# Pooled attention and two gated layers on one core: the first pair's stack is built in place, and three groups of transfers and conversions change their places

## The chip, the cores and the metric

One core of a Trainium2 chip runs the whole program in one launch. The metric is the device time of one execution in microseconds (us); lower is better. The kernel before was timed in three runs, and a fourth execution was taken by the hardware profiler.

## What is computed

Inputs are q, k, v of shape (4, 8, 1152, 64) and two pairs of weight matrices. The reference, cut to what matters:

```python
q_pool = q.reshape(B, H, S // 2, 2, D).mean(axis=3)          # 576 pooled queries per head
scores = scale * matmul(q_pool, k^T)                          # 576 x 1152 per head
scores = scores - max(scores, axis=-1)
attn = exp(scores); attn = attn / (sum(attn) + 1e-09)
x = matmul(attn, v), laid out as 2304 tokens x 512
h = x @ w1_in;  x = (h - tanh(h)) @ w1_out                    # 512 -> 2048 -> 512
h = x @ w2_in;  y = (h * sigmoid(1.702 * h)) @ w2_out         # the same shape
```

## The kernel before, in words

**Attention.** The 32 heads are taken as 16 pairs (`NPAIR`), two heads (s = 0 and 1) to a pair. Of each operand a rounded high part and the rest, the low part, are kept, so that a product is made of three matmuls. Each head has a *stack*, one of three buffers `stacks[h % 3]` = (a1, a2, q2, q3): a1 holds the high part of k on partitions 0 to 63 and the low part on 64 to 127, a2 the high part of k with a row of ones, q2 the high part of the pooled q twice, q3 its low part and, as its 65th row, the negated row of maxima. `stack(p, s)` (L308) fills the four with six transfers on SP's queue, 1296 KB in all, out of the pair's tiles kh, kl, qh, ql.

A pair is 18 steps (`NS`), a head 9 of them, one for each 128 keys. Step g issues `scores(g)` (four matmuls, L392 and L393; the last kind reads a2 and q3 and with it the row of maxima), two exponentials on ACT (L398 and L408; only the first in every third step, which is called whole), the subtraction of the high from the full probabilities on DVE or POOL (`rest`, L416), and `pv(g - 3)` (L428, L438). Beside these run the maxima of the next pair (`max_tile`, L324 on PE and L328 on DVE), which `max_rows(p, s)` (L345) transposes on DVE into `tt` and writes with four small transfers into q3. `prep_*`, `load_*`, `sums`, `merge`, `spread` and `normalise` are hung on steps by the tables `plan` and, for pair 0, `opening`. An entry (o, i): job means: at step i of a pair, do it for the pair o further on. All engines and queues run in the order in which the program issues. SP takes its transfers in that order, and one that waits holds those behind it.

**The opening.** Pair 0 has nobody ahead of it. Its q and k come in halves of 64 partitions. `first_max` (L331) makes the maxima of head 0 in five tiles ahead of step 0 (three matmuls of 384 columns and one reduction of 1152 each), then one whole tile of head 1. The other four tiles of head 1 are cut into halves of 576, eight in all, at steps 0 to 2. `keep_warm` (L566) puts matmuls between whose result nobody reads. `sum_q(1)` (L279), which needs the load of pair 1's q, stands at step 0 on DVE, and `prep_qs(2)`, which needs that of pair 2's, at step 5.

**The two layers** are 80 steps of 24 + 24 matmuls (L691 and L786): 2 layers x 4 quarters of the weights x 5 blocks of tokens (384, 512, 512, 512, 384) x 2. `gate` (L715) makes the activation on ACT and DVE, and `split_g(n)` (L697) splits it into a high part on ACT and a low part, on POOL in layer 0 and on DVE in layer 1. The weights come as 64-bit numbers: each of the 8 pieces of a quarter is converted by four DVE instructions (L137, L143, L150, L157) and one split. The table `turn`, or `usual`, names the step in which a piece is converted (`cv`) and split (`sp`); its load is issued two steps earlier. `split_x` (L112) splits the input blocks of a layer.

Of the kernel before, what the change touches and what calls it, by code (L numbers as in the profile page):

```python
# [28 lines left out]
def tile_pooled_attention_two_moe(  # L29
# [14 lines left out]
    D = 64  # L44
# [166 lines left out]
    def attention(ctx: ExitStack):  # L211
# [119 lines left out]
        def first_max(s, j, x, pool, parts, n):  # L331
            d = pairs[0]
            r = slice(64 * s, 64 * s + 64)
            m = min(128, SP - 128 * j)
            mx = pool.tile([128, parts, 512], F32, tag="mx", name="mx")
            for a in range(parts):
                k0 = (x * parts + a) * n
                nc.tensor.matmul(
                    mx[0:m, a, 0:n], d["qh"][r, 128 * j:128 * j + m], d["kh"][r, k0:k0 + n],
# [5 lines left out]
        def max_rows(p, s, queues=(nc.sync,) * 4):  # L345
# [7 lines left out]
            elif s == 1:  # L353
                nc.vector.tensor_tensor(
                    mt[:, 6:10], f32(mt[:, 6:10]), f32(mt[:, 22:26]), op=ALU.min)
# [13 lines left out]

        def prep_v(p, s):  # L370
            vr = vraw.pop((p, s))
            vr = vr.rearrange("p (m r) d -> p m r d", r=2)
            vh, vl = (outer(x) for x in vt[(2 * p + s) % 3])
            nc.sync.dma_start(
                out=vfs[(2 * p + s) % 3][:, :, 0:D],
                in_=v[p // NPB, p % NPB][:, s, 2 * KG:KT])
# [142 lines left out]
        load_q(0, [low])  # L519
        load_k(0, [low])  # L520
        load_q(0, [high])
        load_k(0, [high])
        load_k(1)
        fill(0)
        new_pair(0)
        d0 = pairs[0]

        def q_sum(eng, out, r):
            eng.tensor_add(d0[out][r], qraw[0][r, 0], qraw[0][r, 1])

        def k_high(eng, r, x):
            c = slice(x * SP, (x + 1) * SP)
            if eng is nc.scalar:
                eng.activation(d0["kh"][r, c], kraw[0][r, c], AF.Copy)
            else:
                eng.tensor_scalar(
                    out=d0["kh"][r, c], in0=kraw[0][r, c],
                    scalar1=1.0, scalar2=1.0, op0=ALU.mult, op1=ALU.mult)

        def k_low(r, x):  # L540
            c = slice(x * SP, (x + 1) * SP)
            nc.gpsimd.tensor_tensor(
                d0["kl"][r, c], kraw[0][r, c], f32(d0["kh"][r, c]), op=ALU.subtract)

        q_sum(nc.vector, "qh", low)
        k_high(nc.scalar, low, 0)
        k_high(nc.gpsimd, low, 1)
        q_sum(nc.vector, "qs", low)
        nc.vector.tensor_sub(d0["ql"][low], d0["qs"][low], f32(d0["qh"][low]))
        k_low(low, 0)  # L550
        k_low(low, 1)
        stack(0, 0)
        k_high(nc.scalar, high, 0)
        k_high(nc.scalar, high, 1)
        q_sum(nc.gpsimd, "qs", high)
        refill(1)
        nc.scalar.activation(d0["qh"][high], d0["qs"][high], AF.Copy)
        k_low(high, 0)
        k_low(high, 1)
        nc.gpsimd.tensor_tensor(  # L560
            d0["ql"][high], d0["qs"][high], f32(d0["qh"][high]), op=ALU.subtract)
        with (tc.tile_pool(name="ps_first", bufs=2, space=PSUM) as ps_first,
              tc.tile_pool(name="ps_warm", bufs=1, space=PSUM) as ps_warm):
            warm = ps_warm.tile([128, 512], F32, name="warm")

            def keep_warm(n):  # L566
                for _ in range(n):
                    nc.tensor.matmul(
                        warm, bdqs[1][:, 0:128], bdqs[1][:, 0:512], start=True, stop=True)
# [16 lines left out]
        prep_v(0, 1)  # L586
        prep_kl(1, 0)
        prep_kl(1, 1)
        load_v(1, 0)
        load_v(1, 1)  # L590
        load_k(2)
        nc.gpsimd.memset(f32(bdqs[0][:]), 0.0)
# [304 lines left out]
```

## Time and profile before

| | |
|---|---|
| three timed runs | 1322.97, 1324.94 (median), 1329.85 us |
| the profiled execution | 1328.51 us, of it 1326.7 us between first and last instruction |
| PE busy | 1297.1 us, 98% of the span |
| DVE, ACT, POOL busy | 988.9, 750.6 and 360.5 us |
| mean granted TensorE clock | 0.992 |
| DMA | 117.57 MB moved |

The span falls into an opening (to about 17 us no scores are made), the attention (to about 522 us) and the two layers (to the end). PE is TensorE's matmuls, PEld its weight loads, DVE VectorE, ACT ScalarE, POOL GpSimd, SP SyncE, which issues most transfers. A `q` behind an engine's name is its sequencer. In a timeline row stand the start, the duration, engine, line, operation, and in brackets how long the engine stood idle before it and for whom.

### The profile page before, as it was taken

What the parts mean: (1) busy time and instruction counts of PE and PEld (TensorE: products, weight loads), DVE (VectorE), ACT (ScalarE), POOL (GpSimd) and SP (SyncE); (2) the same over time, 40 slices, a digit from 0 to 9 for tenths busy, and PEclk for the clock granted to TensorE, in tenths of its full rate; (3) what the DMA queues carried; (4) which work ended last, traced back from release to release, by engine and by line L of the source; (5) the groups of instructions that cost most, each with busy time, mean ns of one, the idle gap of its engine ahead of it and who ended that gap; (6) DMA issues with size and microseconds to landing.
All of it is one profiled execution on the core that took longest, in us unless ns stands there. A gap on an engine that the chain in (4) does not pass through costs nothing.

```text
span 1326.7 us, 18918 instructions
## 1 busy us (share of the span) xinstructions
PE 1297.1 (98%) x7036; PEld 1156.0 (87%) x7036; DVE 988.9 (75%) x1279; ACT 750.6 (57%) x1151; POOL 360.5 (27%) x273
## 2 busy tenths in 40 slices
PE   7899999999999999999999999999999999999998
PEld 5799999999999998888879879889888888889887
DVE  6577877788888878998999999999844546545433
ACT  4567777777677767866666566665544322322211
POOL 4633333224344414223333332323210110110000
PEclk8899999999999999999999999999999999999999
DMA  8777666777877641111111110111211111211012
GB/s 175 182 165 165 149 148 154 173 184 160 186 168 169 160 116 35 42 48 48 48 48 33 48 48 32 49 31 41 72 33 32 53 43 34 62 33 32 24 40 80
DMA packets 59162, 117.57 MB, mean 89 GB/s; under 512 B 25024, under 2 KB 29120, under 8 KB 59072
## 3 DMA queue, kind: packets, MB, share of 16 engines
q1 hardware_dynamic: 59044, 116.38, 35.1%
q8 instruction: 55, 0.90, 0.3%
q14 instruction: 35, 0.29, 0.1%
q10 hardware_dynamic: 28, 0.00, 0.0%
HBM read 66.58 MB, written 4.79 MB: 54 GB/s over the span
## 4 chain that ended last, share of the span: by engine, by line
PE 65%; DVE 16%; DMA 9%; ACT 6%; issue 3%; POOL 1%; SPq 1%; DVEq 0%; POOLq 0%; ACTq 0%
PE y L786 20%; PE h L691 19%; PE pv L438 8%; PE pv L428 5%; PE sc L393 4%; PE sc L392 4%; PE mx L324 4%; DMA kr<-in_k_dram 2%; DVE gg L749 2%; DMA q<-ql 2%; DMA a<-kh 2%; DVE wt L143 2%; DVE wt L137 2%; DVE xb L799 2%; ACT u L730 2%
## 5 line engine op out<-in xcount | busy, mean ns | idle before, releaser
L328 DVE TENSOR_REDUCE mt<-mx 128x1 fp32r<-128x576 f32 x270 | 203.7, 755 | 92.5 <-PE mx L324 88.1
L398 ACT ACTIVATE pf<-sc 128x576 f32<-128x576 f32 x288 | 188.6, 655 | 141.5 <-PE sc L393 130.5
L691 PE MATMUL h<-hl,big 128*128 128x512 f32 (+1 forms) x940 | 211.6, 377 | 0.0
L691 PEld LDWEIGHTS h<-hl,big 128*128 128x128 f32 x940 | 174.0, 188 | 28.5
L392 PE MATMUL sc<-q,big 128*128 128x288 f32 x576 | 185.5, 335 | 0.7 <-ACT ph L408 0.7
L786 PE MATMUL y<-g,big 128*128 128x512 f32 (+1 forms) x780 | 177.7, 370 | 4.5 <-POOL g L703 4.3
L393 PE MATMUL sc<-q,a 65*128 65x288 f32 x576 | 165.8, 301 | 7.4 <-DMA q<-tt 7.4
L786 PE MATMUL y<-big,g 128*128 128x512 f32 x702 | 172.2, 390 | 0.0
L786 PEld LDWEIGHTS y<-g,big 128*128 128x128 f32 x780 | 141.8, 188 | 27.5 <-POOL g L703 8.2
L703 POOL TENSOR_TENSOR g<-gg,g 128x1024 fp32r<-128x1024 f32 (+1 forms) x40 | 88.2, 2205 | 280.7 <-ACT g L701 280.7
L701 ACT ACTIVATE g<-gg 128x1024 fp32r<-128x1024 f32 (+1 forms) x80 | 77.9, 974 | 139.0 <-DVE gg L762 76.1
L786 PEld LDWEIGHTS y<-big,g 128*128 128x128 f32 x702 | 131.7, 188 | 27.1
L438 PE MATMUL pv<-ph,big 128*128 128x288 f32 x768 | 142.3, 296 | 0.5 <-ACT u L444 0.5
L799 DVE TENSOR_TENSOR xb<-xb,y 128x512 f32<-128x512 f32 (+1 forms) x114 | 72.2, 657 | 86.8 <-PE y L786 86.8
L416 DVE TENSOR_TENSOR pl<-pf,ph 128x576 fp32r<-128x576 f32 x159 | 131.1, 824 | 0.6 <-POOL ph L405 0.6
L691 PE MATMUL h<-hl,w 128*128 128x512 f32 (+1 forms) x564 | 127.0, 377 | 0.0
L324 PE MATMUL mx<-kh,big 128*128 128x288 f32 x540 | 117.5, 299 | 5.7 <-DVE mt L328 5.7
L393 PEld LDWEIGHTS sc<-q,a 65*128 65x128 f32 x576 | 110.5, 192 | 14.5 <-issue 5.6
L408 ACT ACTIVATE ph<-sc 128x576 fp32r<-128x576 f32 x188 | 122.9, 654 | 0.0
L691 PEld LDWEIGHTS h<-hl,w 128*128 128x128 f32 x564 | 104.4, 188 | 17.1
L165 POOL TENSOR_TENSOR big<-wt,big 128x512 fp32r<-128x512 f32 x46 | 63.4, 1382 | 205.6 <-ACT big L164 205.6
L438 PEld LDWEIGHTS pv<-ph,big 128*128 128x128 f32 x768 | 116.5, 189 | 1.0 <-issue 0.9
(95 smaller groups left out, 2154.8 us busy)
## 6 DMA issues: line engine op xcount, KB each, us to landing
raw<-in_moe_w_in_dram SPq DMA_DIRECT2D x32, 512.0 KB
raw<-in_moe_w_out_dram SPq DMA_DIRECT2D x32, 512.0 KB
big<-kh SPq DMA_DIRECT2D x32, 288.0 KB
q<-qh SPq DMA_DIRECT2D x64, 144.0 KB
big<-kl SPq DMA_DIRECT2D x32, 288.0 KB
a<-kh SPq DMA_DIRECT2D x32, 288.0 KB
kr<-in_k_dram SPq DMA_DIRECT2D x15, 576.0 KB
qr<-in_q_dram SPq DMA_DIRECT2D x15, 576.0 KB
```

The source lines that it names most:

```text
L324: nc.tensor.matmul(mx[:, a, 0:n], bdqs[p % 2][:, 128 * j:128 * j + 128], d["kh"][:, k0:k0 + n], start=True, stop=True)
L328: nc.vector.tensor_reduce(d["mt"][:, c:c + 1], mx[:, :, 0:n], AX.XY, ALU.max, negate=True)
L392: nc.tensor.matmul(sc[:, x, 0:HB], a1[:, ks], q2[:, xs], start=True, stop=False)
L393: nc.tensor.matmul(sc[:, x, 0:HB], a2[:, ks], q3[:, xs], start=False, stop=True)
L398: nc.scalar.activation(both(pf), sc[:, :, 0:HB], AF.Exp, scale=SCALE)
L408: nc.scalar.activation(both(ph), sc[:, :, 0:HB], AF.Exp, scale=SCALE)
L416: eng.tensor_tensor(pl, pf, f32(ph[:]), op=ALU.subtract)
L438: nc.tensor.matmul(accs[hd][x], w[:, t, :], r[:, x * HB:(x + 1) * HB], start=(t == 0 and n == 0), stop=(t == KT - 1 and n == 2))
L691: nc.tensor.matmul(hb[:, j, 0:TBS[b]], wi[:, c, w, :], x[r][c], start=(k == 0), stop=(k == 3 * NKC - 1))
L703: eng.tensor_tensor(gt[:, :, 1, :], g, f32(gt[:, :, 0, :]), op=ALU.subtract)
L786: nc.tensor.matmul(ys[m][:, 0:w], lhsT, rhs, start=(fp == 0 and k == 0), stop=(fp == 1 and k == 5))
L799: nc.vector.tensor_add(dst, dst, ys[m][:, 0:w])
```

## The change

1. Pair 0's head 0: the engines write a1, a2, q2 and q3 themselves (the low half of k and the copy of q cross from partitions 0 to 63 to 64 to 127), and `stack(0, 0)` with its six transfers goes. ACT gets two more instructions for it.
2. Pair 0's v is loaded ahead of k of pair 1, one piece of 96 KB on ACT's queue; the clearing of `bdqs[0]` moves to the start of POOL's work.
3. Two whole tiles of head 1 stand ahead of step 0, not one; of the other three, six halves stand at steps 0 to 3. 14 warm matmuls become 7. `prep_kh(1)` moves behind the rows of maxima. `sum_q(1)` moves from step 0 to 1, `max_rows(0, 1)` from 3 to 4, `prep_qs(2)` and what follows from it from step 5 to 9.
4. In every pair the third part of v (`prep_v_whole`, 96 KB) for s = 1 moves from step 12 to 15, the load of the next v (192 KB) from 12 to 14, and `spread` (two transfers of 144 KB) from 12 to 14. `max_rows` stays at 13, so that it is ahead of these in SP's order.
5. In the layers, four of the first eight conversions stand one to three steps earlier (the first at step 3 in place of 4), the last `split_g` of layer 0 goes from POOL to DVE, and `split_x` of block 2 moves one step back. `turn[NQ + 1]` and the `max(...)` give the values that were there before.

The diff, cut to its core:

```diff
+            a1, _, q2, _ = stacks[0]
+            lhs, rhs = (q2, a1) if s == 0 else (d["qh"], d["kh"])
...
+        def prep_v_whole(p, s, queue=nc.sync):
+            queue.dma_start(
+                out=vfs[(2 * p + s) % 3][:, :, 0:D],
+                in_=v[p // NPB, p % NPB][:, s, 2 * KG:KT])
+
         def prep_v(p, s):
+            prep_v_whole(p, s)
+            prep_v_split(p, s)
...
+        load_v(0, 0)
+        prep_v_whole(0, 0, nc.scalar)
         load_k(1)
+        load_v(0, 1)
         fill(0)
+        nc.gpsimd.memset(f32(bdqs[0][:]), 0.0)
...
-        q_sum(nc.vector, "qh", low)
-        k_high(nc.scalar, low, 0)
-        k_high(nc.gpsimd, low, 1)
...
-        k_low(low, 0)
-        k_low(low, 1)
-        stack(0, 0)
...
+        q_sum(nc.vector, q2[low], low)
+        k_high(nc.scalar, a1, low, 0)
+        k_high(nc.gpsimd, a1, low, 1)
+        q_sum(nc.vector, d0["qs"][low], low)
+        nc.vector.tensor_sub(q3[low], d0["qs"][low], f32(q2[low]))
+        k_low(a1, high, low, a1, 0)
+        k_low(a1, high, low, a1, 1)
+        k_high(nc.scalar, d0["kh"], high, 0)
+        k_high(nc.scalar, d0["kh"], high, 1)
+        q_sum(nc.gpsimd, d0["qs"][high], high)
+        nc.scalar.activation(a2[low], kraw[0][low], AF.Copy)
+        nc.scalar.activation(q2[high], d0["qs"][low], AF.Copy)
         refill(1)
         nc.scalar.activation(d0["qh"][high], d0["qs"][high], AF.Copy)
...
             new_pair(1)
-            prep_kh(1, 0)
-            prep_kh(1, 1)
             max_rows(0, 0, (nc.sync, nc.scalar, nc.sync, nc.scalar))
-            first_max(1, 0, 0, ps_first, 3, 384)
-            keep_warm(14)
-        load_v(0, 0)
-        prep_v(0, 0)
+            for j in range(2):
+                first_max(1, j, 0, ps_first, 3, 384)
+            keep_warm(7)
+        prep_kh(1, 0)
+        prep_kh(1, 1)
+        prep_v_split(0, 0)
         load_q(1)
         stack(0, 1)
-        load_v(0, 1)
         prep_v(0, 1)
...
         plan = {
             (1, 2): [(stack, 0)], (1, 3): [(prep_v, 0)], (1, 10): [(stack, 1)],
-            (1, 12): [(prep_v, 1)], (1, 13): [(max_rows, 0)], (0, 3): [(max_rows, 1)],
+            (1, 12): [(prep_v_split, 1)], (1, 13): [(max_rows, 0)], (1, 15): [(prep_v_whole, 1)],
+            (0, 3): [(max_rows, 1)],
...
-            (2, 12): [(load_v, 1)], (2, 14): [(prep_ql,)],
+            (2, 14): [(prep_ql,), (load_v, 1)],
...
         opening = {
-            (0, 3): [(max_rows, 1, (nc.sync, nc.scalar, nc.sync, nc.sync))],
-            (1, 0): [(sum_q,)], (2, 0): [(load_q,)], (1, 1): [(prep_bdq, 0)],
+            (0, 4): [(max_rows, 1, (nc.sync, nc.scalar, nc.sync, nc.sync))],
+            (1, 1): [(sum_q,)], (1, 2): [(prep_bdq, 0)], (1, 3): [(prep_bdq, 1), (prep_qh,)],
+            (2, 1): [(load_q,)], (1, 4): [(prep_ql,)],
...
-            (2, 5): [(prep_qs,)], (2, 6): [(prep_qh,)], (2, 7): [(prep_bdq, 0)],
+            (2, 9): [(prep_qs,)], (2, 10): [(prep_qh,)], (2, 11): [(prep_bdq, 0)],
...
-                elif i == 12:
+                elif i == 14:
                     spread(p - 1)
...
-            eng = nc.gpsimd if li == 0 else nc.vector
+            eng = nc.gpsimd if n < NQ * 2 * NB - 1 else nc.vector
...
-            1: (("i", 0, 4, 5), ("i", 1, 5, 6), ("o", 0, 6, 7), ("i", 2, 7, 9), ("i", 3, 8, 9),
-                ("o", 1, 9, 10), ("o", 2, 10, 11), ("o", 3, 11, 12)),
+            1: (("i", 0, 3, 4), ("i", 1, 4, 5), ("o", 0, 5, 6), ("o", 1, 6, 7),
+                ("i", 2, 7, 9), ("i", 3, 8, 9), ("o", 2, 10, 11), ("o", 3, 11, 12)),
...
-                at(NQ * 2 * NB + (c - 7, c - 4, c // 2 - 1, c // 2 + 2, c // 2 + 4)[b],
+                at(NQ * 2 * NB + (c - 7, c - 4, c // 2, c // 2 + 2, c // 2 + 4)[b],
                    "end", lambda b=b, c=c: split_x(b, [c], nc.vector))
```

## Rows read from the trace of the kernel before

**Rows 1.** Windows of 5 us: busy us of PE, PEld, DVE, ACT, POOL, clock, DMA, GB/s.

```profile
25.00:30.00 5.00, 2.85 (x10) 2.21 (x10) 3.56 (x6) 1.40 (x3) 0.00 (x0) 0.50 1.05 196
30.00:35.00 5.00, 5.00 (x19) 4.36 (x18) 3.19 (x7) 3.57 (x6) 2.69 (x3) 0.50 0.34 66
...
45.00:50.00 5.00, 4.57 (x19) 4.00 (x20) 2.41 (x4) 2.40 (x5) 0.00 (x0) 0.61 0.73 199
50.00:55.00 5.00, 5.00 (x37) 4.79 (x36) 2.97 (x5) 4.50 (x8) 1.43 (x1) 1.00 0.99 208
```

**Rows 2.** The timeline of PE in the opening: the rows with idle time before them.

```profile
19.46 0.37 PE L393 MATMUL sc<-q,a 65*128 65x288 f32 x1 [1.57 <-DMA q<-tt]
...
27.14 0.85 PE L338 MATMUL mx<-kh,qh 64*128 64x288 f32 x2 [2.50 <-DVE mt L342]
...
45.43 0.85 PE L324 MATMUL mx<-kh,big 128*128 128x288 f32 x2 [5.70 <-DVE mt L328]
```

**Rows 3.** The timeline of the other engines in the same stretch.

```profile
6.77 3.22 POOL L542 TENSOR_TENSOR kl<-kr,kh 64x576 fp32r<-64x576 f32 x2
...
12.54 0.66 ACT L557 ACTIVATE qh<-qs 64x576 fp32r<-64x576 f32 x1
...
14.98 2.18 ACTq L367 DMA_DIRECT2D q<-tt  x2
...
25.66 0.76 DVE L280 TENSOR_TENSOR qs<-qr 128x576 f32<-128x576 f32 x1 [2.74 <-DMA qr<-in_q_dram]
...
35.38 0.38 SPq L257 DMA_DIRECT2D qr<-in_q_dram  x1
...
43.16 1.55 DVE L280 TENSOR_TENSOR qs<-qr 128x576 f32<-128x576 f32 x1 [5.55 <-DMA qr<-in_q_dram]
```

**Rows 4.** Groups by form in the first 60 us: count, busy us, mean ns.

```profile
L342 DVE TENSOR_REDUCE mt<-mx 128x1 fp32r<-128x1152 f32 x5 | 6.5, 1352 | 1.1 <-PE mx L338 1.0
...
L342 DVE TENSOR_REDUCE mt<-mx 128x1 fp32r<-128x576 f32 x6 | 4.4, 753 | 4.6 <-PE mx L338 4.6
```

**Rows 5.** The chain that ended last, in order of time: start, duration, what.

```profile
17.55 8.02 DMA qr<-in_q_dram
...
84.54 8.76 DMA a<-kh
93.31 0.61 SPq L367
93.97 1.58 DMA q<-tt
```

**Rows 6.** PE's waits from 60 to 520 us: total, times, longest.

```profile
PE sc L393 <- DMA q<-tt: 5.8, 7, 1.4
```

**Rows 7.** The timeline of PE at two pair boundaries.

```profile
95.68 0.37 PE L393 MATMUL sc<-q,a 65*128 65x288 f32 x1 [0.66 <-DMA q<-tt]
...
340.98 0.40 PE L393 MATMUL sc<-q,a 65*128 65x288 f32 x1 [1.41 <-DMA q<-tt]
```

**Rows 8.** A window of 10 us ahead of a boundary, columns as in the first group.

```profile
80.00:90.00 10.00, 10.00 (x70) 9.58 (x69) 7.72 (x14) 7.77 (x15) 1.73 (x3) 1.00 1.01 240
```

**Rows 9.** PE's waits from 480 us to the end.

```profile
PE y L786 <- POOL g L703: 5.3, 9, 1.7
```

**Rows 10.** The timeline of PE in the layers: the longest wait but one.

```profile
628.44 4.26 PE L786 MATMUL y<-g,big 128*128 128x384 f32 x23 [1.16 <-POOL g L703]
```

**Rows 11.** The timeline of ACT and POOL at the change of layers.

```profile
929.61 0.85 ACT L701 ACTIVATE g<-gg 128x768 fp32r<-128x768 f32 x1
...
930.53 2.40 POOL L703 TENSOR_TENSOR g<-gg,g 128x768 fp32r<-128x768 f32 x1 [6.70 <-ACT g L701]
```

**Rows 12.** Groups by form from 880 to 960 us.

```profile
L137 DVE TENSOR_SCALAR wt<-raw 128x512 int32<-128x512 int32 x8 | 7.9, 982 | 0.0
...
L150 DVE SCALAR_TENSOR_TENSOR wt<-wa,wt 128x512 f32<-128x512 f32 x8 | 5.5, 693 | 0.8
...
L703 DVE TENSOR_TENSOR g<-gg,g 128x768 fp32r<-128x768 f32 x2 | 3.0, 1501 | 0.0
```

More of the change, by code (lines that the diff above doesn't have):

```diff
@@ L518, in attention @@
         low, high = slice(0, 64), slice(64, 128)
[L519 to L522, printed above, removed]
+        load_q(0, low)
+        load_k(0, low)
+        load_q(0, high)
+        load_k(0, high)
+        load_v(0, 0)
+        prep_v_whole(0, 0, nc.scalar)
         load_k(1)
+        load_v(0, 1)
         fill(0)
+        nc.gpsimd.memset(f32(bdqs[0][:]), 0.0)
         new_pair(0)
         d0 = pairs[0]
+        a1, a2, q2, q3 = stacks[0]
@@ L528, in q_sum, with half, k_high @@
         def q_sum(eng, out, r):
-            eng.tensor_add(d0[out][r], qraw[0][r, 0], qraw[0][r, 1])
-        def k_high(eng, r, x):
-            c = slice(x * SP, (x + 1) * SP)
+            eng.tensor_add(out, qraw[0][r, 0], qraw[0][r, 1])
+        def half(t, r, x):
+            return t[r, x * SP:(x + 1) * SP]
+        def k_high(eng, out, r, x):
+            o, i = half(out, r, x), half(kraw[0], r, x)
             if eng is nc.scalar:
-                eng.activation(d0["kh"][r, c], kraw[0][r, c], AF.Copy)
+                eng.activation(o, i, AF.Copy)
@@ L545, in attention @@
-        q_sum(nc.vector, "qh", low)
-        k_high(nc.scalar, low, 0)
-        k_high(nc.gpsimd, low, 1)
-        q_sum(nc.vector, "qs", low)
-        nc.vector.tensor_sub(d0["ql"][low], d0["qs"][low], f32(d0["qh"][low]))
-        k_low(low, 0)
-        k_low(low, 1)
-        stack(0, 0)
-        k_high(nc.scalar, high, 0)
-        k_high(nc.scalar, high, 1)
-        q_sum(nc.gpsimd, "qs", high)
+                half(out, to, x), half(kraw[0], r, x), f32(half(hi, r, x)), op=ALU.subtract)
+        q_sum(nc.vector, q2[low], low)
@@ L556, in attention @@
         refill(1)
         nc.scalar.activation(d0["qh"][high], d0["qs"][high], AF.Copy)
-        k_low(high, 0)
-        k_low(high, 1)
+        k_low(d0["kl"], high, high, d0["kh"], 0)
+        k_low(d0["kl"], high, high, d0["kh"], 1)
         nc.gpsimd.tensor_tensor(
             d0["ql"][high], d0["qs"][high], f32(d0["qh"][high]), op=ALU.subtract)
-        with (tc.tile_pool(name="ps_first", bufs=2, space=PSUM) as ps_first,
-              tc.tile_pool(name="ps_warm", bufs=1, space=PSUM) as ps_warm):
-            warm = ps_warm.tile([128, 512], F32, name="warm")
+        with (tc.tile_pool(name="ps_warm", bufs=1, space=PSUM) as ps_warm,
+              tc.tile_pool(name="ps_first", bufs=2, space=PSUM) as ps_first):
+            warm = ps_warm.tile([128, 2, 512], F32, name="warm")
@@ L568, in keep_warm @@
                     nc.tensor.matmul(
-                        warm, bdqs[1][:, 0:128], bdqs[1][:, 0:512], start=True, stop=True)
+                        warm[:, 0], bdqs[1][:, 0:128], bdqs[1][:, 0:512], start=True, stop=True)
             keep_warm(11)
@@ L599, in attention @@
         max_at = {}
-        for h in range(8):
-            max_at.setdefault(h // 3, []).append(
-                lambda h=h: first_max(1, 1 + h // 2, h % 2, ps_mx, 2, HB))
+        for h in range(6):
+            max_at.setdefault((h + 1) // 2, []).append(
+                lambda h=h: first_max(1, 2 + h // 2, h % 2, ps_mx, 2, HB))
         for n in range(1, NPAIR):
@@ L821, in moe @@
                 jobs = joined(piece(kind, qn * 4 + f))
-                for job, w, place in zip(jobs, (cv - 2, cv, cv, sp), places, strict=True):
+                for job, w, place in zip(jobs, (max(cv - 2, 0), cv, cv, sp), places, strict=True):
                     at((qn - 1) * 2 * NB + w, place, job)
```

52 lines of the change are left out of this document (22 added, 30 removed).

## The prediction

> **What bounds the kernel now.** I read the page first, then windows over the span, then PE's waits by stretch. PE is busy for 98% of the span, so a gain can only come from the stretches where it is idle, runs at the lower clock, or does work that nobody reads. There are three. In the opening PE's timeline has three long gaps, 1.57, 2.50 and 5.70 us [rows 2]. Each of the last two stands behind a reduction of maxima on DVE, and DVE itself stood behind `sum_q` or `prep_qs`, waiting 2.74 and 5.55 us for a load of q [rows 3]: an addition that is not urgent holds the reductions behind it in DVE's order, and these hold PE. Around the gaps the clock fell: 0.50 of full (1.2 in place of 2.4 GHz) from 25 to 35 us after the first two, 0.61 between 45 and 50 after the third, and back at 1.00 from 50 once PE had worked without a gap [rows 1]. In the attention PE waits 5.8 us in 7 places, all for the rows of maxima at a pair's start [rows 6]. In the layers it waits 5.3 us in 9 places for the low part of the activation from POOL [rows 9]. Everything else that the change moves lies beside a busy PE and is worth nothing by itself.
>
> **Part 1, the opening: 10.9 us.**
> *First scores, +0.3.* The six transfers of `stack(0, 0)` go; nothing waited for them, so that is free bandwidth only. ACT gets k's high part (64 x 1152, twice a 64 x 576 copy) and the copy of q: 3 x 0.66 = 2.0 us ahead of qh, which then ends at 13.20 + 2.0 = 15.2 [rows 3]. Behind it on ACT wait its two rows of maxima, and on PE the whole tiles of head 1. ACT's two row issues took 2.18 us, from 14.98 to 17.16 [rows 3]. From 15.2 they end at 17.4 if they cost the same, 0.2 later, or at 16.4 if each costs the 0.61 of a later one [rows 5], 0.8 sooner. I take 0.7 sooner, nearest to the repeated row, because another transfer now goes through ACT's queue first. That transfer is the 96 KB of v, which runs beside the first q and k. If it shares the engines with them it costs 96 KB at 240 GB/s [rows 8] = 0.4 us of the chain that leads to the maxima; if not, nothing. I take the 0.4, as the DMA share stands near 1 whenever loads of this size run [rows 1, 8]. (The Trainium skill, "DMA: Bandwidth & Descriptors", section "Issuing engines are not separate DMA queues", says that transfers of all queues run on the same 16 engines and interleave. By that the sum holds; by a queue with room of its own it is 0.4 us better. No row here separates the two.) Bounds: -0.6 to +0.8. The seven warm matmuls that go stand in front of the rows' landing and cost nothing either way.
> *The 2.50 us gap, +2.0.* `load_q(1)` was issued at 17.55 and took 8.02 us to land [rows 5], with 288 KB of v just ahead of it. Now v is loaded earlier, the load goes out about 1 us sooner with only the rows ahead, and its reader stands a step later, behind three more DVE instructions. It could again take 8 us, as six transfers of `stack(0, 1)` still follow it at once; then DVE waits another 1 to 2 us. Bounds 0 to 2.5.
> *One more whole tile ahead of step 0, +1.3.* Two halves of 0.75 us leave steps 0 to 2, where DVE sets the pace, and a whole of 1.35 us [rows 4] goes where PE and DVE wait for the rows anyway: two tiles from about 16.1 end at 18.8, and the first scores ran at 19.46 [rows 2]. Bounds 0 to 1.5.
> *The 5.70 us gap, +5.6.* Before, q of pair 2 was issued at 35.38 and its reader started at 43.16 [rows 3], 7.8 us later. Now it goes out as soon as `sum_q(1)` has freed the buffer, at about 24, and lands by about 32. Its reader is at step 9, which can't come before 34: step 1 at about 21, then eight steps of 1.70, the mean between the two boundaries of [rows 7], which lie eight pairs of 18 steps apart. Bounds 3 to 5.7. What is late next: q of pair 3, whose load moves from step 7 to 10 behind the six transfers of `stack(1, 1)`. 1296 + 576 KB at 240 GB/s are 7.8 us, and its reader is seven steps, 11.9 us, away; it fits.
> *The clock, +1.7.* Without the third gap the second fall should not come. From 45.43 to about 48.9 PE did 3.5 us of work at half clock [rows 1, 2], which is 1.7 at full. The first fall I keep: steps 0 to 4 still move at DVE's pace. If it went too, the 5.00 us of unbroken work from 30 to 35 would shrink by 2.5; another stretch of that length costs 2.5. Bounds -0.8 to +4.2.
> The other moves of this part (`bdqs[0]` cleared early on POOL, `prep_kh(1)` later, `max_rows(0, 1)` at step 4, `prep_qs(2)`'s followers) cost nothing: POOL and ACT are idle where they go, and heads 1 to 4 need them several steps later.
>
> **Part 2, rows ahead of other transfers: 4.8 us.** Four transfers of 96 + 192 + 2 x 144 = 576 KB leave the place between a stack and the rows. At 240 GB/s [rows 8] that is 2.4 us, more than the longest of the seven waits, 1.41 [rows 7]. At one boundary the last row's issue began when the stack's a<-kh had landed, at 93.31, and the row landed at 95.5; PE had been ready at 95.0 [rows 5, 7]. Without the four the issues come up to 2 us earlier. But the data still queue behind a<-kh, so a short rest can stay: I take five sixths of 5.8. Bounds 0 (the rows can't pass a<-kh) to 5.8. The moved ones have three to six steps more until they are read, and cost nothing as long as the queue drains between a pair's end and its step 2.
>
> **Part 3, the layers: 2.5 us.** At the change of layers POOL's 2.40 us split ends at 932.93, having begun when ACT's copy ended [rows 11]; PE waits the longest of its nine waits there, 1.7 us [rows 9]. DVE does the form in 1.50 [rows 12], 0.9 less, and `split_x` of block 2 no longer stands near it: 1.0 us (0.5 to 1.7). The other eight waits are 3.6 us, the longest, 1.16, at 628 us [rows 10], behind a run of steps with a conversion each. A conversion is 0.98 + 3 x 0.69 = 3.1 us of DVE [rows 12]. The change takes one off step 9 and puts one on step 3. I take 1.5; if DVE is full from step 3 on, it only moves the waits forward (0, or 1 lost). Bounds -1 to 3.3.
>
> **Sum.** 10.9 + 4.8 + 2.5 = 18.2 us. The profiled execution took 1328.51, so it would take 1310.3; it stands 3.6 above the median of the timed runs, 1324.94, from which the same sum gives 1306.7, say 1307. About 0.5%, 6.6 us, is what a measurement here can tell from no change.
>
> **Rivals.**
> *The stall moves.* q of pair 1 lands as late as before and the lower clock holds longer: the opening gives 4 in place of 10.9, so 1314. For it: the 8.02 us landing. Against: 288 KB less ahead of it.
> *The rows can't pass a<-kh.* Part 2 gives nothing: 1312. For it: that issue at 93.31. Against: 576 KB less in the queue.
> *The clock stays up*, and parts 2 and 3 come out near their best: 1301.
> *Parts cancel.* Opening 4, nothing else: 1321, no measurable change. Two of the edits do nothing by their own numbers (`turn[NQ + 1]` repeats the usual row).
> *Slower: POOL writing across partitions.* No row shows POOL reading partitions 0 to 63 and writing 64 to 127. Unshifted, the two instructions start at 6.77 and take 1.61 each [rows 3]; the far end is a whole stack transfer, 8.76 [rows 5]. Step 0 needs them by 19.2, so up to 6.2 each costs nothing, and 8.76 costs 5 us (1312). From 15.3 each the whole gain is gone; at 20 the time is 1335. Against: nothing near 15 us exists in the rows for so little data. (The Trainium skill, "GPSIMD Engine Reference", section "5.1 Two access paths", says that in ordinary elementwise work every core keeps to its own 16 partitions. By that such an instruction is no ordinary one, but no price is given, and no row here shows one.)
>
> **Chances.** The forecast 0.57 (1303 to 1311), the stall moves 0.14, rows held 0.11, the clock stays up 0.08, parts cancel 0.06, POOL 0.04. Faster by over 0.5%: 0.57 + 0.14 + 0.11 + 0.08 = 0.90; within: 0.06; slower: 0.04. The range 1297 to 1317 takes in the first four with their bounds.
>
> **What would show it.** Step by step in the profile after: no gap over 1 us on PE between 27 and 50 us, and a clock that falls at most once; `sum_q(1)` and `prep_qs(2)` on DVE without a wait over 1.5 us; the two POOL instructions at about 1.6 us each; PE's waits for the rows under 1.5 us in all, not 5.8; at the change of layers a wait under 0.8 us; waits for the low part under 3 us in all. The prediction is wrong if scores of step 9 still start after 45 us, or if the rows' waits stay above 4 us.

## The result and the profile after

Four runs after took 1311.86 to 1312.42 us, median 1312.17; four runs before beside them 1322.97 to 1329.85, median 1325.45. The ratio is 0.9896, with a 95% interval of 0.987 to 0.9923: faster by 1.0%, by more than the 0.5% that a measurement here can tell. The forecast was 1307 in 1297 to 1317. The profiled executions went from 1328.51 to 1311.86, 16.65 us less, where the sum of the steps was 18.2; the two medians lie 13.3 us apart.

Where the time went is read from five places in PE's timeline: the first matmul of the scores of steps 0, 5 and 11, the first matmul of the layers, and the end of the span (us).

| | step 0 | step 5 | step 11 | layers | end | step 11 to layers | layers to end |
|---|---|---|---|---|---|---|---|
| before | 17.59 | 35.63 | 53.14 | 522.55 | 1326.7 | 469.41 | 804.2 |
| after | 20.81 | 35.46 | 45.69 | 508.04 | 1310.1 | 462.35 | 802.1 |
| gained up to there, or in the stretch | -3.2 | 0.2 | 7.45 | | 16.6 | 7.06 | 2.1 |

So part 1 gave 7.45 us (forecast 10.9), part 2 gave 7.06 (4.8) and part 3 gave 2.1 (2.5). The first three terms of the opening (0.3 + 2.0 + 1.3 = 3.6) gave 0.2 by step 5; the last two (5.6 + 1.7 = 7.3) gave 7.3 between steps 5 and 11. The row "before" is one profile. Two more of the same opening (e8 and e5 below) came to step 5 at 34.24 and 33.59 and to step 11 at 50.81 and 50.37; against them part 1 gave 5.1 and 4.7, and its first three terms lost 1.2 and 1.9.

PE's waits after, from 0 to 60 us (total, times, longest):

```profile
PE mx L338 <- ACT qh L570: 2.3, 1, 2.3
PE warm L581 <- DVE big L230: 2.1, 1, 2.1
PE sc L399 <- DMA q<-tt: 0.6, 1, 0.6
...
```

Both long gaps of [rows 2] are gone; a wait for qh of 2.3 us ahead of step 0 is new. PE's waits after from 470 us to the end:

```profile
PE y L798 <- ACT xb L809: 3.5, 3, 1.8
PE y L798 <- POOL g L715: 1.5, 3, 0.8
...
```

The seven waits for the rows [rows 6] have no line left: from 60 to 515 us PE has three waits of 0.4 to 0.7, none for `tt`. In the layers the wait for POOL [rows 9] fell from 5.3 to 1.5, and one for ACT's `xb` came.

Windows of 5 us after (busy us of PE, PEld, DVE, ACT, POOL, clock, DMA, GB/s):

```profile
15.00:20.00 5.00, 4.86 (x12) 3.93 (x13) 2.62 (x2) 1.34 (x3) 4.40 (x5) 0.50 0.65 158
20.00:25.00 5.00, 4.26 (x12) 2.51 (x10) 0.76 (x1) 1.19 (x2) 0.21 (x1) 0.50 1.01 203
25.00:30.00 5.00, 5.00 (x17) 3.79 (x16) 4.07 (x6) 2.53 (x4) 4.88 (x6) 0.50 0.97 245
30.00:35.00 5.00, 4.91 (x18) 4.10 (x18) 2.40 (x5) 3.21 (x5) 0.03 (x1) 0.50 0.30 115
35.00:40.00 5.00, 5.00 (x34) 4.71 (x33) 3.06 (x6) 2.48 (x5) 1.91 (x2) 0.89 0.14 28
```

Compare with [rows 1]: PE is busy for 4.26 to 5.00 us of every 5 and yet at 0.50 (1.2 GHz) from 15 to 35 us. The second fall, between 45 and 50, is gone, but the first began earlier: in the profile before, the clock was still 1.00 from 10 to 20 us.

```profile
15.00:20.00 5.00, 3.42 (x17) 2.53 (x15) 1.36 (x1) 0.00 (x0) 1.23 (x3) 1.00 0.60 96
```

The timeline after, the rows that answer to [rows 3] and to the steps of the opening (POOL, ACT, ACT's and SP's sequencers, PE, DVE):

```profile
6.76 3.17 POOL L554 TENSOR_TENSOR big<-kr,big 64x576 fp32r<-64x576 f32 x2
...
9.96 1.17 ACT L567 ACTIVATE a<-kr 64x1152 fp32r<-64x1152 f32 x1
11.14 0.68 ACT L568 ACTIVATE q<-qs 64x576 fp32r<-64x576 f32 x1
...
14.17 1.54 ACTq L367 DMA_DIRECT2D q<-tt  x1
14.42 0.66 ACT L570 ACTIVATE qh<-qs 64x576 fp32r<-64x576 f32 x1
...
15.74 0.60 ACTq L367 DMA_DIRECT2D q<-tt  x1
...
15.81 0.37 SPq L256 DMA_DIRECT2D qr<-in_q_dram  x1
...
28.88 0.33 SPq L256 DMA_DIRECT2D qr<-in_q_dram  x1
...
15.14 2.29 PE L338 MATMUL mx<-kh,qh 64*128 64x384 f32 x6 [2.34 <-ACT qh L570]
17.35 3.35 PE L581 MATMUL warm<-big 128*128 128x512 f32 x7
20.81 0.58 PE L398 MATMUL sc<-q,big 128*128 128x288 f32 x1
22.03 0.58 PE L399 MATMUL sc<-q,a 65*128 65x288 f32 x1 [0.63 <-DMA q<-tt]
...
28.11 0.74 DVE L278 TENSOR_TENSOR qs<-qr 128x576 f32<-128x576 f32 x1
...
44.22 0.82 DVE L278 TENSOR_TENSOR qs<-qr 128x576 f32<-128x576 f32 x1
```

and a piece of the chain that ended last, after (start, duration, what):

```profile
15.74 6.04 DMA q<-tt
21.78 0.25 issue
22.03 0.58 PE sc L399
```

Three things are to be seen. `sum_q(1)` at 28.11 and `prep_qs(2)` at 44.22 have no wait in brackets, and q of pair 2 is issued at 28.88, not 35.38. The two additional ACT instructions took 1.85 us (forecast 2.0) and qh ended at 15.08 (forecast 15.2), but PE stood 2.34 us for it, and the tiles of head 1 and the seven warm matmuls behind them ran at half clock and ended at 20.7. And the last row on ACT's queue, issued from 15.74 to 16.34, landed at 21.78.

What held q of pair 2 before is in SP's timeline of the kernel before, just ahead of the row at 35.38 [rows 3]:

```profile
26.77 0.39 SPq L374 DMA_DIRECT2D vf<-in_v_dram  x1
27.56 7.25 SPq L267 DMA_DIRECT2D vr<-in_v_dram  x2
34.86 0.42 SPq L263 DMA_DIRECT2D kr<-in_k_dram  x1
```

The two loads of pair 1's v took SP 7.25 us to issue: in that stretch SP waited 4.3 us for pair 0's v to land and 2.3 for POOL, which splits it. All loads behind stood in the same line.

### The profile page after: what moved, and what is told of

Same layout as the page of the kernel before. It is cut to its first block, busy times and chain, and to the rows that moved or that the text cites. A ratio compares the mean times of both kernels' runs of the same rounds, so it can differ in the third digit from the quotient of the medians.

```text
span 1310.1 us, 18881 instructions
## 1 busy us (share of the span) xinstructions
PE 1293.6 (99%) x7028; PEld 1155.3 (88%) x7028; DVE 990.8 (76%) x1279; ACT 752.7 (57%) x1153; POOL 361.4 (28%) x272
## 4 chain that ended last, share of the span: by engine, by line
PE 75%; DVE 14%; ACT 6%; issue 3%; DMA 1%; POOL 1%; SPq 0%; DVEq 0%; ACTq 0%; POOLq 0%
PE y L798 21%; PE h L703 20%; PE pv L444 11%; PE pv L434 7%; PE sc L399 5%; PE mx L322 5%; PE sc L398 5%; DVE gg L761 2%; DVE wt L137 1%; DVE wt L143 1%; DVE xb L811 1%; ACT u L742 1%; DVE wt L150 1%; DVE gg L744 1%; DVE wt L157 1%
## 5 line engine op out<-in xcount | busy, mean ns | idle before, releaser
L398 PEld LDWEIGHTS sc<-q,big 128*128 128x128 f32 x576 | 110.8, 192 | 7.8 <-issue 1.7
```

The source lines that it names most:

```text
L398: nc.tensor.matmul(sc[:, x, 0:HB], a1[:, ks], q2[:, xs], start=True, stop=False)
```

## The experiments

The experiments were timed in three groups, each beside seven runs of the kernel before, whose medians there were 1329.41, 1328.33 and 1329.1 (1324.82 to 1332.76 over all). Ratios are to these.

**All four rows of head 0 on SP (e1).**

```diff
-            max_rows(0, 0, (nc.sync, nc.scalar, nc.sync, nc.scalar))
+            max_rows(0, 0)
```

> The kernel after, but the four rows of maxima of pair 0's first head all go through SP's queue, where they stand ahead of the load of pair 1's q. In the kernel after the last of ACT's two rows took 6.04 us to land (issued at 15.74, landed at 21.8), and step 0's second kind of matmul waited for it until 22.03. Theory 1, the row on ACT's queue is overtaken by the q load that SP issues at 15.81: the rows land by about 19 and that matmul follows its predecessor at about 21.4 without a wait, step 11 starts up to 0.6 us earlier than 45.69, time 1311.5 (1311 to 1312.2). Theory 2, the 6 us are the time that any such row needs there: the matmul still starts at 22 or later, time 1312.2 to 1313.

Measured 1309.17 us (1308.84 to 1309.21), ratio 0.9849 (0.9823 to 0.9874): 3.0 less than after, more than was expected. Rows of e1's timeline, SP and PE:

```profile
15.73 2.86 SPq L367 DMA_DIRECT2D q<-tt  x4
...
18.70 0.38 SPq L256 DMA_DIRECT2D qr<-in_q_dram  x1
...
20.78 0.38 PE L398 MATMUL sc<-q,big 128*128 128x288 f32 x1
21.01 0.37 PE L399 MATMUL sc<-q,a 65*128 65x288 f32 x1
```

The rows go out ahead of the load of q, and nothing waits for them. Step 0 starts where it did (20.78 for 20.81), but step 5 at 31.83 and step 11 at 42.63, 3.1 earlier than after. The second kind of matmul of step 0 comes 1.0 us sooner (21.01 for 22.03); the larger share lies behind it, where the clock was 0.93 from 20 to 25 us in place of 0.50:

```profile
20.00:25.00 5.00, 4.83 (x24) 3.09 (x22) 2.42 (x4) 2.52 (x5) 0.00 (x0) 0.93 0.98 219
```

Why it rose sooner is not separated from the missing wait.

**qh ahead of the copy of q on ACT (e2).**

```diff
         nc.scalar.activation(a2[low], kraw[0][low], AF.Copy)
+        nc.scalar.activation(d0["qh"][high], d0["qs"][high], AF.Copy)
         nc.scalar.activation(q2[high], d0["qs"][low], AF.Copy)
         refill(1)
-        nc.scalar.activation(d0["qh"][high], d0["qs"][high], AF.Copy)
```

> The kernel after, but on ACT the rounding of q's high half (qh, which the whole tiles of head 1 need) stands ahead of the copy of q2 and of the refill. Theory 1, ACT's order alone made PE idle for 2.34 us before 15.14: the gap shrinks to under 0.5 us and head 1's tiles start at about 12.3, but step 0 still waits for the late row at 22, so step 11 and the time stay (1311.8 to 1312.5). Theory 2, that gap is also what put the clock to 1.2 GHz from 12.2 to 36.1 us: with PE busy without a break the clock stays at 2.4 GHz until past 15 us and step 11 comes 2 to 4 us earlier, time 1308 to 1310.

Measured 1311.84 us (1311.6 to 1313.24), ratio 0.9871 (0.9846 to 0.9897): no difference from after. The wait for qh went, step 0 started at 19.34, and what was late next stood there. PE's timeline in e2:

```profile
22.96 0.58 PE L399 MATMUL sc<-q,a 65*128 65x288 f32 x1 [3.03 <-DMA q<-tt]
```

So with the row on ACT's queue the wait for qh costs nothing by itself: the row holds step 0 in any case.

**Both (e3).** The two diffs above together.

> Both: all four rows on SP's queue and qh first on ACT. Theory 1, the first three terms of my sum (3.6 us) were given back by the late qh and the late row together: step 0's second kind of matmul starts at 19 or before in place of 22.03, step 11 is 2.5 to 3.5 us earlier than 45.69, time 1308.5 to 1309.8. Theory 2, DVE's reductions or the half clock set the pace of steps 0 to 5 whatever their start: step 0 is earlier, but step 11 by less than 1.5 us, time 1311 or more.

Measured 1307.93 us (1307.69 to 1308.23), ratio 0.984 (0.9815 to 0.9865), 4.2 less than after and the lowest median of all kernels here. Step 0 is at 19.30 and step 11 at 41.67, 4.0 earlier. What is left in e3's windows:

```profile
20.00:25.00 5.00, 4.47 (x24) 3.04 (x22) 3.84 (x6) 3.23 (x6) 0.00 (x0) 1.00 1.01 225
25.00:30.00 5.00, 3.86 (x15) 3.48 (x16) 3.74 (x4) 3.31 (x6) 2.75 (x2) 0.53 1.08 232
```

With steps 0 to 2 at full clock PE runs into DVE again: a gap behind the reduction that follows `sum_q(1)`, and a low clock after it.

```profile
26.14 0.74 PE L338 MATMUL mx<-kh,qh 64*64 64x288 f32 x2 [1.61 <-DVE mt L342]
```

**The reader of q of pair 2 back at step 5 (e4).** Was it the place of `prep_qs(2)` or the time of its load that closed the 5.70 us gap?

```diff
-            (2, 9): [(prep_qs,)], (2, 10): [(prep_qh,)], (2, 11): [(prep_bdq, 0)],
-            (2, 12): [(prep_bdq, 1)], (2, 13): [(prep_kh, 0), (load_v, 0)],
+            (2, 5): [(prep_qs,)], (2, 6): [(prep_qh,)], (2, 7): [(prep_bdq, 0)],
+            (2, 8): [(prep_bdq, 1)], (2, 13): [(prep_kh, 0), (load_v, 0)],
```

> The kernel after, but pair 2's sum over q (prep_qs) and its three followers stand at steps 5 to 8 again, as before. Theory 1, the 5.70 us gap went because the load of that q now goes out at 28.9 (before 35.4, SP having been held by loads of v that waited for POOL), and by step 5 at about 35.4 it has landed: no wait of DVE for it over 0.5 us, step 11 within 0.5 us of 45.69, time 1311.8 to 1312.7. Theory 2, it went because the reader moved four steps back: DVE waits several us at step 5, PE behind it, time 1315 to 1318.

Measured 1311.25 us (1311.11 to 1312.44), ratio 0.9867 (0.9837 to 0.9898): the same as after. The load goes out at 28.60 and its reader runs at 37.51 without a wait. The place of the reader gives nothing; the load does.

**Part 2 alone (e5)**, in the kernel before: `prep_v` in two, and in the tables

```diff
-            (1, 12): [(prep_v, 1)], (1, 13): [(max_rows, 0)], (0, 3): [(max_rows, 1)],
+            (1, 12): [(prep_v_split, 1)], (1, 13): [(max_rows, 0)], (1, 15): [(prep_v_whole, 1)],
+            (0, 3): [(max_rows, 1)],
...
-            (2, 12): [(load_v, 1)], (2, 14): [(prep_ql,)],
+            (2, 14): [(prep_ql,), (load_v, 1)],
...
-                elif i == 12:
+                elif i == 14:
                     spread(p - 1)
```

> The kernel before with the second part alone: the third part of v at step 15, the load of the next v and the spread at step 14, all behind the rows of maxima in SP's order. From the scores of step 11 to the first matmul of the layers the kernel before takes 469.4 us (53.14 to 522.55) and the kernel after 462.4 (45.69 to 508.04). Theory 1, all 7.1 us of that come from the rows' place in SP's order: this stretch takes 462.0 to 462.8 and PE waits less than 0.5 us for the rows, time some 7 us under the kernel before, beside which it runs. Theory 2, the opening's new phase gave part of it: the stretch takes 464 or more and rows are still waited for.

Measured 1318.59 us (1317.81 to 1318.8), ratio 0.9925 (0.9907 to 0.9943). From step 11 to the layers it takes 461.90 us (50.37 to 512.27), 7.5 less than before; the layers take 803.8 (before 804.2). PE's one wait from 60 to 505 us in e5:

```profile
PE pv L444 <- ACT u L450: 0.5, 1, 0.5
```

From 60 to 505 us PE was busy 439.10 of 445 us before and now 444.37. The seven gaps of PE, 5.8 us, were worth 7.5: PEld stood longer at the same seven places, 7.3 us in all (1.65 where PE's gap was 1.41 at 340.98 [rows 7]). In every kernel here with part 2 the stretch from step 11 to the layers took 461.9 to 462.7 us, in every one without it 469.4 to 470.7.

**The change without part 3 (e6):** POOL for the last `split_g`, the old `turn[1]`, the old first entry of `usual`, `split_x` of block 2 one step forward.

```diff
-            eng = nc.gpsimd if n < NQ * 2 * NB - 1 else nc.vector
+            eng = nc.gpsimd if n < NQ * 2 * NB else nc.vector
...
-            ("i", 0, 1, 2), ("o", 1, 3, 4), ("i", 1, 4, 5), ("o", 0, 5, 6),
+            ("i", 0, 2, 3), ("o", 1, 3, 4), ("i", 1, 4, 5), ("o", 0, 5, 6),
```

> The kernel after with the whole third part undone: conversions at their old steps (also the first piece of every later quarter, step 2 in place of 1), the last low part of layer 0 on POOL, split_x of block 2 as before. From the first matmul of the layers to the end the kernel before takes 804.2 us, the kernel after 802.1. Theory 1, the part is worth just that: the stretch takes 803.8 to 804.5, PE waits over 5 us for POOL's low parts and under 0.3 us for ACT's copies of y, 1.7 us of it at the change of layers, time 1314 to 1314.6. Theory 2, the waits come from how the attention ends and not from these edits: the stretch stays at 802 to 803, time 1312 to 1313.

Measured 1314.0 us (1313.36 to 1314.48), ratio 0.9891 (0.9873 to 0.9909), with the layers at 803.9. PE's waits in the layers of e6:

```profile
PE y L798 <- POOL g L715: 5.3, 9, 1.7
```

That is the total, the count and the longest wait of [rows 9]. Part 3 is worth 1.9 us in the layers; from step 11 to the layers e6 takes 462.4, as after.

**Only the first entry of `usual` back (e9).** This entry had been overlooked in the prediction (below).

```diff
-            ("i", 0, 1, 2), ("o", 1, 3, 4), ("i", 1, 4, 5), ("o", 0, 5, 6),
+            ("i", 0, 2, 3), ("o", 1, 3, 4), ("i", 1, 4, 5), ("o", 0, 5, 6),
```

> The kernel after with one edit undone, one that my prediction overlooked: the first piece of each later quarter is converted at step 2 again, not 1. With 1 it falls on step 11 of the quarter before, where another piece is converted: in the kernel after ACT's second conversion at 625.53 stood 3.66 us for DVE, ACT's copies of y came behind it, and PE waited 1.76 us at 627.36. Theory 1, that collision costs what PE waited: the wait at that step is under 0.3 us and the layers take 800.2 to 801.2 in place of 802.1, time 1310.3 to 1311.3. Theory 2, DVE is full in this stretch, and the piece only delays something else: waits for POOL's low parts come back around 640 to 680, the layers take 801.7 or more, time 1311.8 to 1313.

Measured 1311.91 us (1311.87 to 1312.05), ratio 0.9876 (0.9854 to 0.9897). The layers take 801.5, 0.5 less than after. PE's waits in the layers of e9:

```profile
PE y L798 <- POOL g L715: 2.3, 6, 0.8
PE y L798 <- ACT xb L809: 1.7, 2, 1.5
...
PE y L798 <- DVE g L715: 0.3, 1, 0.3
```

Beside the two rows of after (3.5 and 1.5), half of the wait for `xb` goes and smaller waits come: the earlier first conversion is no gain.

**Less to do around the start (e7, e10, e11).** Three tries on top of e3. e7 shortens the warm matmuls and moves the sum and the next load a step later; e10 lengthens the warm matmuls and has e9's `usual`; e11 has e7's move with seven warm matmuls, and e9's `usual`.

```diff
-            keep_warm(7)
+            keep_warm(4)
...
-            (1, 1): [(sum_q,)], (1, 2): [(prep_bdq, 0)], (1, 3): [(prep_bdq, 1), (prep_qh,)],
-            (2, 1): [(load_q,)], (1, 4): [(prep_ql,)],
+            (1, 2): [(sum_q,), (prep_bdq, 0)], (1, 3): [(prep_bdq, 1), (prep_qh,)],
+            (2, 2): [(load_q,)], (1, 4): [(prep_ql,)],
```

(e10 has `keep_warm(10)` and the `opening` of after; e11 keeps `keep_warm(7)`.)

> The run with both (rows on SP's queue, qh first), and besides the sum over pair 1's q one step later (step 2) and 4 warm matmuls in place of 7. In that run the rows had landed before the warm matmuls ended at 19.05, and PE waited 1.61 us at 26.14 behind the sum. Theory 1, both are on the path: step 0 is 0.6 to 1.3 us earlier, step 11 0.8 to 2 us earlier than 41.67, time 1306 to 1307.1. Theory 2, DVE's reductions of steps 0 to 3 are the path, or fewer warm matmuls let the clock fall for longer: step 11 not earlier, time 1307.7 or more.

> The run with both (rows on SP's queue, qh first), 10 warm matmuls in place of 7, and the first piece of the later quarters at step 2 (worth 0.5 us of the layers: 801.5 in place of 802.1). With 4 warm matmuls step 0 came at 17.70 but the clock stayed low from 15.3 to 32.4 and step 11 came at 42.20; with 7 step 0 came at 19.30, the clock was back at 18.5, and step 11 came at 41.67. Theory 1, the clock after step 0 matters more than when step 0 starts: with 10, step 0 comes at about 20 to 20.6, the clock is low for no longer than 10 us in all, and step 11 is within 0.5 us of 41.67, time 1307 to 1307.8. Theory 2, the seven were enough and each one more is lost on PE: step 11 at 42.2 to 43, time 1308 to 1308.7.

> The run with both, 7 warm matmuls, the first piece of the later quarters at step 2, and the sum over pair 1's q at step 2 in place of 1. Theory 1, that sum stands 0.7 to 0.8 us in front of two reductions which PE waited 1.61 us for at 26.14: without it that wait shrinks by 0.7, step 11 comes up to 0.8 us earlier than 41.67, time 1306.6 to 1307.3. Theory 2, the sum has to be done before the maxima of pair 1 at step 4, and its two copies on ACT and the load of pair 2's q only come later: step 11 at 41.5 to 42.3, time 1307.3 to 1308.

e7: 1308.67 us (1308.04 to 1309.14), ratio 0.9851 (0.9833 to 0.9869). Step 0 starts at 17.70, 1.6 earlier than in e3, and step 11 at 42.20, 0.5 later. Its window

```profile
20.00:25.00 5.00, 5.00 (x16) 3.89 (x17) 2.84 (x4) 2.30 (x4) 0.00 (x0) 0.50 1.00 224
```

has PE busy throughout and at half clock, where e3 had full clock and gaps. e10: 1308.37 us (1308.15 to 1308.56), ratio 0.9841 (0.9819 to 0.9862), step 0 at 20.31 and step 11 at 42.86. e11: 1308.48 us (1306.98 to 1310.85), ratio 0.9838 (0.9811 to 0.9864); its runs lie 3.9 us apart, and its profile is of the longest of them (1310.85), with the clock at 0.50 from 10 to 32.5 us and step 11 at 45.4. The shortest, 1306.98, is below every run of e3, so e11 decides nothing. By the medians none beats e3.

**Pair 0's v early, and nothing else (e12)**, in the kernel before: the stack of head 0 is still written by transfers.

```diff
         load_k(0, [high])
+        load_v(0, 0)
         load_k(1)
+        load_v(0, 1)
...
-        load_v(0, 0)
         prep_v(0, 0)
...
-        load_v(0, 1)
         prep_v(0, 1)
```

> The kernel before with one move: both loads of pair 0's v stand at the start, ahead of and behind the load of pair 1's k. Theory 1, the 5.70 us gap came from SP's order: in the kernel before the load of pair 2's q was issued at 35.38 only, because SP stood at a load of v until POOL had split the v before it, and that v had been loaded at 25.6. With v early SP is not held, that q goes out by about 28, has landed when step 5 asks for it, PE's gap near 45 is under 1 us, step 11 comes 4 to 7 us earlier than 53.14 (50.37 in another run with this opening), time 4 to 7 us under the kernel before. Theory 2, SP is held by something else (the six transfers of the second stack, the sum over pair 1's q): the q goes out after 33, the gap stays over 3 us, time within 2 us of the kernel before.

Measured 1320.04 us (1317.87 to 1320.9), ratio 0.9926 (0.9902 to 0.995): 9 us less than before. The profile is of the shortest of its four runs, 2.2 us under the median. Rows of e12's timeline (SP, DVE, PE):

```profile
26.57 0.33 SPq L257 DMA_DIRECT2D qr<-in_q_dram  x1
...
34.97 0.75 DVE L280 TENSOR_TENSOR qs<-qr 128x576 f32<-128x576 f32 x1
...
24.22 0.85 PE L338 MATMUL mx<-kh,qh 64*128 64x288 f32 x2 [2.04 <-DVE mt L342]
...
43.02 0.51 PE L392 MATMUL sc<-q,big 128*128 128x288 f32 x1
```

SP no longer stands for v, the load of q of pair 2 goes out 8.8 us sooner, its reader at step 5 finds it, and the gap of 5.70 us is gone. The 2.50 us gap stays (2.04). Step 11 is at 43.02: 10.1 us earlier than before, and 2.7 earlier than after, which has this and all the rest of part 1. From step 11 to the layers it takes 469.6 us (before 469.4) and in the layers 803.5 (804.2).

**The kernel before once more (e8)**, without an edit, since its runs lie 10 us apart (1322.97 to 1332.76) and those of after 0.6.

> The kernel before once more, for a second profile of it. Its timed runs spread over 8 us (1324.8 to 1332.8), those of the same kernel with the rows ahead of the other transfers over 1 us. Theory 1, the spread comes from the waits for rows: in this profile the opening to step 11 is within 3 us of 53.14, the layers take 804.2 again, and what differs in the span is the stretch from step 11 to the layers, 469.4, and PE's 5.8 us of waits in it. Theory 2, it comes from the clock in the opening: that stretch stays within 0.7 us and step 11 differs.

Its profiled execution took 1327.37 us, 1.1 less than the profile ahead of the prediction. Step 11 was at 50.81, 2.3 earlier; from there to the layers it took 470.67, 1.3 longer; the layers 804.1, the same to 0.1. So its spread lies in the opening and in the waits for the rows, the two places where PE waits for a landing. PE's gaps of 2.50 and 5.70 us [rows 2] were these in e8:

```profile
26.31 0.84 PE L338 MATMUL mx<-kh,qh 64*128 64x288 f32 x2 [4.31 <-DVE mt L342]
...
43.13 0.60 PE L324 MATMUL mx<-kh,big 128*128 128x288 f32 x2 [4.79 <-DVE mt L328]
```

e5, whose program is that of the kernel before up to step 11, gives a third profile of this opening. There the clock had fallen before 15 us, the 14 warm matmuls took 5.96 us in place of 3.48 and step 0 came at 20.69, `sum_q(1)` found its q landed, the two gaps were 0.94 and 3.56 us, and step 11 came at 50.37. Its windows:

```profile
15.00:20.00 5.00, 5.00 (x12) 3.94 (x13) 1.35 (x1) 0.00 (x0) 1.88 (x3) 0.50 0.65 136
20.00:25.00 5.00, 4.09 (x21) 2.95 (x20) 3.00 (x5) 1.92 (x4) 0.28 (x1) 0.97 0.99 233
```

Gains below 2.5 us in the opening are therefore told here from kernels with steady runs, not from one profile of the kernel before.

## Why the prediction was right, and where not

**The verdict and the size.** Faster by over 0.5% was right, and 1312 lies in the range, 5 us above the forecast. Of these 5, 3.6 come from the base: the sum was taken from the median of three runs, 1324.94, and not from the profiled execution, whose own figure of 1310.3 was 1.6 from the profile of after. The later medians of the kernel before, 1328.3 to 1329.4, suggest that the profiled execution was the usual one, though the four runs beside after had 1325.45. The other 1.6 are three errors that partly cancel: 3.4 too much in the opening, 2.3 too little for the rows, 0.4 too much in the layers. That the sum of the steps came so near is in part luck. All the signs that the prediction named for the profile came true, but none of them looked at the start of step 0, where its opening failed.

**First scores, +0.3: wrong, and the failed step of the opening.** ACT's additional work and the end of qh came out as worked out. So did the end of ACT's row issues (16.34, forecast 16.4), but by luck: they did not stand behind qh. The first began at 14.17, ahead of qh, and the two took 2.17 us, as before (2.18), not twice 0.61. Two things in the step failed. "Nothing either way" for the seven warm matmuls held only while PE had nothing else behind qh: PE stood 2.34 us for qh, then ran the tiles and the warm matmuls at half clock, 0.48 us for each warm matmul (before 0.25), and could not start step 0 before 20.8. And the row on ACT's queue was priced up to its issue alone. It landed 5.4 us after that: the load of q, 576 KB, had been issued on SP at 15.81, while the row's issue ended at 16.34. Before, only the 288 KB of v went out beside ACT's last row, SP's load of q followed it (17.55 after 17.16), and the row had landed 2.3 us after its issue. So the same edit that the next term counts as a gain, the load of q going out sooner, put that load beside a row that everything waits for. e2 shows the row alone to be enough to hold the start; e1, with the rows moved, is 3.0 us faster, and e3, with qh first as well, 1.2 more. (The Trainium skill, "DMA: Bandwidth & Descriptors", section "Issuing engines are not separate DMA queues", has it that transfers interleave on the same engines whichever engine issued them. The 6.04 us agree: a queue of its own gave the row no way past. e1 changes the queue and the order at once, so it doesn't tell which of them counts.) The late start is not by itself the loss. Step 0 started at 20.81 in after, 20.78 in e1 and 20.69 in e5, but the clock from 20 to 25 us was 0.50, 0.93 and 0.97, and step 5 came at 35.46, 31.83 and 33.59. The prediction kept the first fall of the clock as it was; in after it began earlier and held to 36 us, and why it did is not shown.

**The 0.4 for v on ACT's queue** was not seen: the first q is read at 4.73 (before 4.65) and the first k at 5.92 (6.00).

**The 2.50 us gap and the whole tile, +2.0 and +1.3.** The gap is gone, as forecast, and `sum_q(1)` waits for nothing; but the same gap was 4.31 in e8 and 0.94 in e5, so what its end is worth depends on the profile it is taken from. In after that worth is hidden by the late start; in e3, where the start is in time, a gap of 1.61 us stands at the same place, for DVE's order and not for a load. What these terms gave back went into the start and the half clock, and step 5 came only 0.2 us earlier.

**The 5.70 us gap and the clock, +5.6 and +1.7: right**, 7.3 between steps 5 and 11 (6.3 against e8, 6.6 against e5), and no second fall of the clock. The reason was half right. The prediction had the load wait for `sum_q(1)`, which after the change is so (28.85 and 28.88); before it waited behind the loads of pair 1's v on SP, and these for pair 0's v. e12 shows that loading pair 0's v early closes the gap by itself, and e4 that the reader's move to step 9 is idle. With one reservation, as e8 shows that a profile of the kernel before may differ by 2.3 us here: e12 gains 10.1 in the opening against the first profile and 7.8 against e8, and either is more than the 7.45 (5.1 against e8) of all of part 1. e12's profile is of its shortest run; by the medians it gains 9 us.

**Rows ahead, 4.8: right in the mechanism, too small.** All seven waits are gone in after and in e5, so the rows were not held by a<-kh, and this rival falls. The term was capped at 5.8, the sum of PE's gaps, and that cap failed: the stretch became 7.1 us shorter in after and 7.5 in e5. In this trace the gaps on PE's row, whose ends are modelled, were less than the delay that the waits made: 5.8 us on PE at the seven places, 7.3 on PEld.

**The layers, 2.5.** The change of layers was to give 1.0 and gave 1.6: from the first matmul of step 40 to that of step 42 it took 18.65 us before, 17.08 after and 18.68 in e6. The row of after that answers to [rows 11] is

```profile
915.42 0.96 DVE L715 TENSOR_TENSOR g<-gg,g 128x768 fp32r<-128x768 f32 x1 [0.43 <-ACT g L713]
```

where the price was 1.50, a mean of two instructions [rows 12]; after, the three from 880 to 960 us took 0.96, 2.05 and 2.06, and the one that counts was the short one. The conversions gave 0.3 (e6) to 0.6, not 1.5: this term was mis-sized. Waits for POOL of 3.8 us went, 1.7 of them at the change of layers, but PE got 3.5 us of new ones for `xb`, none of which e6 has: 1.8 at 627, and 1.7 in two places at 564 and 587, which stay in e9 and so belong to the other edits of part 3. After, ACT and PE at 627:

```profile
625.53 0.67 ACT L136 ACTIVATE wa<-raw 128x512 f32<-128x512 f32 x1 [3.66 <-DVE wt L150]
...
626.84 0.47 ACT L809 ACTIVATE xb<-y 128x384 f32<-128x384 f32 x1
...
627.36 1.90 PE L798 MATMUL y<-g,big 128*128 128x384 f32 x9 [1.76 <-ACT xb L809]
```

ACT's part of a conversion waits 3.66 us for DVE, and the copy of y that PE needs stands behind it on ACT. Here lies an error in the text on record: it says that `turn[NQ + 1]` repeats the usual row, and the section on the change says that this table and the `max(...)` give the values that were there before. The `max(...)` keeps the load at step 0, but the table does so for one quarter only. The new `usual` begins with `("i", 0, 1, 2)` and not `("i", 0, 2, 3)`, so that in the four quarters that use it the first conversion stands a step earlier, beside the last of the quarter before. e9 takes this back: half of the wait for `xb` goes, and the layers are 0.5 us shorter in its profile (the timed runs of e9 and after overlap). The entry was missed, not mispriced.

**The rivals.** POOL across partitions, the slower one, is out: two instructions in 3.17 us, 3.22 before [rows 3]. (By the Trainium skill, "GPSIMD Engine Reference", section "5.1 Two access paths", an ordinary elementwise instruction keeps to each core's own partitions; the row shows no price for leaving them.) "The stall moves" came true in its second half: no q was late, but the low clock held from before 15 to 36 us, and the opening gave 7.5, between its 4 and the forecast's 10.9. "The clock stays up" didn't come, and its 1301 was not the sum of its own bounds: with the clock, the rows and the layers all at their best it is 1302.4. The two marks named as making the prediction wrong, step 9 after 45 us and row waits above 4 us, did not appear: step 11 is at 45.69, step 9 ahead of it at 42.53, and the waits are gone.

## What to carry over

An early load pays through what it lets go behind it in its queue: look for the transfer that waits for a buffer and count everything that stands after it; here two loads of 192 KB, moved, gave at least as much as the whole rebuilt opening (e3, the rebuilt opening with its start repaired, came to step 11 1.4 us before e12). When a large load is moved forward, look for a tiny transfer of another queue that would be issued beside it, as its landing and not its issue is what counts. And a gap on the matmul row is not the worth of a stall. The seven waits for rows, with nothing else behind them, were worth more (7.1 to 7.5 us for 5.8, and 7.3 on the weight loads); the wait for qh, with a late row behind it, was worth nothing in e2.

The best kernel found is the changed one with all four rows on SP and qh first (e3), 1307.93 us, 4.2 under after. As an estimate from the stretches, e12 with e5 and part 3 alone, with no stack built in place, would end at 1316.1 - 7.7 - 1.9 = 1306.5 us of span, where e3 has 1306.1; from e12's median it would be 2.2 more. That was not run.

## What was not expected of the hardware

A transfer of 0.6 KB took 6.04 us from issue to landing while a load of 576 KB, issued beside it, was in flight, and PE stood 3.03 us for one in e2. e1 and e3, with the rows on SP ahead of that load, have no such wait.

TensorE's clock fell to 1.2 GHz with PE busy. In e7 PE was busy for 5.00 of 5.00 us from 20 to 25 at a granted 0.50; in e3, in the same window, PE had gaps and 1.00. The first fall came before 12.5 us in after (0.94 from 10 to 12.5, where PE was busy 2.44 of 2.50) and not before 20 in the kernel before. In all ten kernels with the changed opening it came before 17.5 us; of the four profiles in which head 0's stack is written by transfers, it came after 20 in three and before 15 in e5. What decides when it falls in the opening stays open: e7 and e10, which change the warm matmuls, move it without a gain, and no kernel here was at full clock throughout.
